# Windowed attention and a rational feed-forward layer: scores as 64x64 products, k and q turned on TensorE in the first steps, and a new order

## The chip, the cores and the metric

The kernel runs on one core of a Trainium2 chip. Time is device microseconds of one execution. A core has TensorE (PE: matrix products out of SBUF into PSUM; PEld is its weight load, which runs beside the products), VectorE (DVE), ScalarE (ACT), GpSimd (POOL) and the sync engine (SP). In this kernel POOL and SP mostly issue transfers: POOL's loads cast from f32 to bf16 on their way, SP issues transfers that transpose. TensorE's clock has two levels, 1.2 and 2.4 GHz; the profile shows the granted clock as a share of the higher one.

## The reference

```python
scores = (1 / sqrt(64)) * q @ k.T              # 4 batches, 8 heads, 768 tokens, 64 wide
keep = (key < 4) | ((0 <= query - key) & (query - key < 128))
a = softmax(where(keep, scores, -1e9))
x = (a @ v)                                    # put back to 3072 tokens x 512
h = x @ w_in                                   # 512 -> 2048
P = a0 + a1*h + a2*h*h + a3*h*h*h
Q = 1 + |b0|*|h| + |b1|*h*h
out = (P / (Q + 1e-6)) @ w_out                 # 2048 -> 512
```

Each query sees at most 128 keys behind it and the first 4 keys, the sink.

## The kernel before, in words

The 3072 tokens are worked in 12 steps of 256 tokens, three to a batch. A step `s` has an attention part and a feed-forward part; the two are apart by some steps, so that all engines have work.

**Attention.** k and q are held transposed, two heads (a pair, `i` = 0 to 3) on the 128 partitions. `scores(s, i)` makes, for each of the four blocks of 64 keys, one product with 192 queries behind it. The keys of the two heads stand block-diagonally in a 128x128 weight (`kT_fix`, half of it zeros), so that both heads come out of one product. For steps 0, 1, 2, 3, 6 and 9 (`PE_MASK`) a second product with the identity as weight adds the negative mask on two edges of 64 columns; in the other steps VectorE multiplies by a mask afterwards (`mask`). `exps` on ScalarE takes 768 columns per pair out of PSUM. There is one PSUM home for scores, `ps_scores` (step 0 borrows a second), so a group of scores waits for the exponentials of the group before. `sink_scores` makes the scores of the sink keys, `attend` the products with v (in 4 groups in step 0 and 3 groups later, called `G`), with a column of ones that gives the softmax sum; `normalize` (`norm`) divides on VectorE.

**How k, q and x are turned.** k and q of most steps are loaded by POOL (`load_k`, `load_q`) and transposed by SP transfers (`turn_k_tile`, `turn_q`). The transposed k lands in `kT_flat`, and VectorE copies it to the block-diagonal tile (`spread_k`, two instructions a step). In step 0 k and part of q are loaded as f32 by SP and ACT queues, cast, turned on TensorE and spread by VectorE and ScalarE; in step 1 k and q are turned on TensorE too. The normalized x is turned on TensorE in steps 0 and 1 (`turn_x`, `place_x`) and by SP transfers later (`turn_x_tile`). V stands in three tiles, one for each step of a batch, and POOL loads it with eight transfers a step.

**Feed-forward.** `project_in` (`gemm1`, four groups of 16 products of 256 columns a step), `copy_in` on ScalarE, and then the rational function on tiles of 4096 columns: `and`, `sqd`, `den`, `even`, `odd`, `odd_h`, `num`, `gate` on VectorE, `sqa`, `ln`, `exp` on ScalarE. Step 0 is worked in 2 parts, step 11 in 4. `project_out` (`gemm2`, four groups of 8 products of 512 columns), `copy_out`, `store`.

**Order.** Every piece of work has a number, and the list `ORDER` is the order in which the pieces are written into the program; each engine runs its pieces in that order. A negative number in the list is that many fillers (`spin`): products of the identity with itself into columns of `ps_scores` that nobody reads. There are 372 of them, 88 behind the first `gemm1` of step 2.

Of the kernel before, what the change touches and what calls it, by code (L numbers as in the profile page):

```python
# [72 lines left out]
def kernel(  # L73
# [13 lines left out]
    nc = tc.nc  # L87
# [20 lines left out]
    MW = NFFC * TS  # L108
    HW = MW // 2
    NQ0 = NTS + 1  # L110
    NS_PE = 2
    GRP = NPB // 2
    HG = H // 2
    CG = HG * D
# [139 lines left out]
    def load_v_sink():  # L254
        nc.scalar.dma_start(out=stage_s, in_=v[0, :, 0:NS, :])
# [791 lines left out]
```

## Time and profile before

| what | value |
|---|---|
| median of 3 runs | 271.79 us (270.04 to 273.13) |
| span of the profiled execution | 275.9 us |
| TensorE busy | 252.4 us (91%) |
| VectorE busy | 225.2 us (82%) |
| ScalarE busy | 221.2 us (80%) |
| GpSimd busy | 118.8 us (43%) |
| mean granted TensorE clock | 0.988 |

The profile shows one execution by its span from the first to the last instruction, and gives no other time for it. That span is 4.1 us longer than the median of the timed runs. Busy time of TensorE counts each product from its start to its modelled end, and neighbours overlap; how long a stream of products takes is read from the chain of waits, where a run of equal products stands with its length and count.

### The profile page before, as it was taken

Reading aid. Unit: us, or ns where it says so; the run is one execution under the profiler, and the core shown is the slowest. Engines: PE = TensorE matmul, PEld = TensorE weight load, DVE = VectorE, ACT = ScalarE, POOL = GpSimd, SP = SyncE. Lnnn points to the kernel's source line nnn. Section 1 sums busy time; section 2 is a strip of 40 time slices with the busy share of each in tenths; the row PEclk is TensorE's granted clock in tenths of the full one; section 3 lists DMA queues with packets and bytes.
Section 4 is the critical chain, followed back from the end, with each engine's and each line's share of the span. In section 5 each row is a group of like instructions: output and inputs, shape, how many; then the busy total and the mean of one; then the engine's idle time right before and its main releaser. Section 6 shows DMA issues by size and latency. Waiting matters only on the chain.

```text
span 275.9 us, 5692 instructions
## 1 busy us (share of the span) xinstructions
PE 252.4 (91%) x2344; PEld 192.4 (70%) x2344; DVE 225.2 (82%) x283; ACT 221.2 (80%) x201; POOL 118.8 (43%) x170
## 2 busy tenths in 40 slices
PE   2978898888599889999999999999999999999994
PEld 2968797777487587787776778777687776655551
DVE  3244318989917978999999999999999999999981
ACT  6084555898259669998989979999998999999870
POOL 8876677598069304083390990698000000000000
PEclk9997999999979999999999999999999999999999
DMA  6999999979999947599699999699901211211022
GB/s 140 192 162 185 117 112 129 137 85 162 118 79 90 124 74 53 130 105 180 80 74 154 124 110 203 45 139 156 122 4 39 77 57 21 76 76 40 26 88 77
DMA packets 113586, 28.72 MB, mean 104 GB/s; under 512 B 104344, under 2 KB 110488, under 8 KB 113560
## 3 DMA queue, kind: packets, MB, share of 16 engines
q0 software_dynamic: 75568, 13.00, 73.6%
q1 hardware_dynamic: 36464, 14.30, 28.8%
q10 hardware_dynamic: 1528, 1.06, 1.3%
q8 instruction: 18, 0.29, 0.5%
q14 instruction: 8, 0.07, 0.1%
HBM read 27.30 MB, written 6.29 MB: 122 GB/s over the span
## 4 chain that ended last, share of the span: by engine, by line
PE 51%; DVE 26%; ACT 12%; issue 6%; DMA 3%; POOL 1%; POOLq 0%
PE ps_out L664 19%; PE ps_h L596 16%; PE ps_s L432 5%; PE ps_o L524 4%; DMA xblk<-x_n 3%; DVE sq L634 3%; ACT lnq L640 3%; ACT e L480 3%; DVE kT L420 3%; DVE g L650 2%; PE ps_s L468 2%; DVE den L617 2%; DVE x_n L548 2%; ACT hb L603 2%; ACT den L645 2%
## 5 line engine op out<-in xcount | busy, mean ns | idle before, releaser
L596 PE MATMUL ps_h<-xblk,w_in_sb 128*128 128x256 bf16 x768 | 91.5, 276 | 2.6 <-DMA xblk<-x_n 2.5
L664 PE MATMUL ps_out<-w_out_sb,g 128*128 128x512 bf16 x368 | 86.3, 379 | 0.6 <-ACT o_t L673 0.3
L596 PEld LDWEIGHTS <-w_in_sb 128*128 128x128 bf16 x768 | 75.2, 99 | 13.5 <-issue 2.2
L238 POOL DMA_DIRECT2D v_bd<-in_v_dram x96 | 66.9, 723 | 37.1 <-PE ps_o L524 22.5
L664 PEld LDWEIGHTS <-g 128*128 128x128 bf16 x384 | 36.8, 98 | 37.2 <-issue 1.0
L603 ACT ACTIVATE hb<-ps_h 128x1024 bf16<-128x1024 f32 x48 | 48.9, 1033 | 12.9 <-PE ps_h L596 12.7
L480 ACT ACTIVATE e<-ps_s 128x768 bf16<-128x768 f32 x48 | 39.1, 816 | 11.9 <-PE ps_s L471 7.9
L640 ACT ACTIVATE lnq<-den,one_eps,qsc 128x4096 f32<-128x4096 bf16 (+2 forms) x16 | 47.2, 2956 | 0.0
L645 ACT ACTIVATE den<-lnq 128x4096 bf16<-128x4096 f32 (+2 forms) x16 | 44.1, 2771 | 0.0
L432 PE MATMUL ps_s<-ident 128*128 128x128 bf16 x372 | 28.1, 233 | 14.5 <-ACT e L480 9.3
L432 PEld LDWEIGHTS <-ident 128*128 128x128 bf16 x372 | 25.6, 106 | 16.7 <-issue 10.4
L230 POOL DMA_DIRECT2D k_bf<-in_k_dram x22 | 20.1, 916 | 35.5 <-DMA kT_flat<-k_bf 35.3
L524 PE MATMUL ps_o<-v_bd,e 128*128 128x130 bf16 x352 | 28.8, 220 | 1.2 <-DVE x_n L548 0.9
L650 DVE TENSOR_TENSOR g<-num,den 128x4096 bf16<-128x4096 bf16 (+2 forms) x16 | 28.0, 1752 | 1.6 <-ACT den L645 1.3
L468 PE MATMUL ps_s<-qT,kT 128*128 128x192 bf16 x192 | 28.1, 248 | 0.1
L621 DVE TENSOR_TENSOR den<-den,sq 128x4096 bf16<-128x4096 bf16 (+2 forms) x16 | 28.0, 1750 | 0.1
L634 DVE TENSOR_TENSOR sq<-sq,hb 128x4096 bf16<-128x4096 bf16 (+2 forms) x16 | 27.9, 1752 | 0.1
L637 DVE TENSOR_TENSOR num<-num,sq 128x4096 bf16<-128x4096 bf16 (+2 forms) x16 | 27.8, 1749 | 0.0
L524 PEld LDWEIGHTS <-e 128*128 128x128 bf16 x352 | 23.7, 97 | 5.2 <-DVE x_n L548 2.6
L610 ACT ACTIVATE sq<-hb 128x2048 bf16<-128x2048 bf16 (+1 forms) x15 | 25.4, 1695 | 0.1
L617 DVE TENSOR_SCALAR den<-hb 128x2048 uint32<-128x2048 uint32 (+2 forms) x16 | 15.9, 992 | 8.7 <-ACT hb L603 8.6
L222 POOL DMA_DIRECT2D q_bf<-in_q_dram x21 | 20.7, 996 | 0.4 <-DMA v_bd<-in_v_dram 0.4
(86 smaller groups left out, 252.4 us busy)
## 6 DMA issues: line engine op xcount, KB each, us to landing
out_dram<-o_t SPq DMA_DIRECT2D x22, 256.0 KB, 2.3
v_bd<-in_v_dram POOLq DMA_DIRECT2D x96, 32.0 KB, 4.6
k_bf<-in_k_dram POOLq DMA_DIRECT2D x22, 128.0 KB, 4.7
q_bf<-in_q_dram POOLq DMA_DIRECT2D x21, 128.0 KB, 5.2
w_in_sb<-in_moe_w_in_dram POOLq DMA_DIRECT2D x4, 512.0 KB, 7.8
w_out_sb<-in_moe_w_out_dram POOLq DMA_DIRECT2D x4, 512.0 KB, 8.1
stage_b<-in_q_dram ACTq DMA_DIRECT2D x2, 384.0 KB, 6.3
stage_a<-in_k_dram SPq DMA_DIRECT2D x2, 256.0 KB, 5.3
```

The costliest lines, as they stand in the source:

```text
L238: nc.gpsimd.dma_start(out=v_bd[s][e * 64:(e + 1) * 64, i, :, e, 0:D], in_=v[b, h, g * TS:(g + 1) * TS, :].rearrange("(j p) d -> p j d", p=64))
L432: nc.tensor.matmul(ps_scores[:, 0, 384:384 + P], lhsT=ident, rhs=ident, start=True, stop=True)
L468: nc.tensor.matmul(w_, lhsT=kT_fix[s % 2][:, i * NHF + n, :], rhs=qT_fix[b % 2][:, i, c:c + 192], start=True, stop=not on_pe)
L480: nc.scalar.activation(out=data.rearrange("p (a n) c -> p a n c", a=2), in_=ps[:, :, 0:384].rearrange("p a (n c) -> p a n c", n=2), func=A ...
L524: nc.tensor.matmul(ps_o[:, u, :], lhsT=l_, rhs=r_.rearrange("p e c -> p (e c)"), start=(m == 0), stop=(m == len(terms) - 1))
L596: nc.tensor.matmul(ps[:, n, :], lhsT=w_in_all[:, c, fc * P:(fc + 1) * P], rhs=xblk[m][:, c, :], start=(c == 0), stop=(c == NDMC - 1))
L603: nc.scalar.activation(out=hb[m][:, j * GW:(j + 1) * GW], in_=ps_h.pop((m, j)).rearrange("p n c -> p (n c)"), func=AF.Copy)
L634: nc.vector.tensor_tensor(out=sq[m][:, c], in0=sq[m][:, c], in1=hb[m][:, c], op=ALU.mult)
L640: nc.scalar.activation(out=lnq_fix[:, c], in_=den[m][:, c], func=AF.Ln, scale=qsc, bias=one_eps)
L645: nc.scalar.activation(out=den[m][:, c], in_=lnq_fix[:, c], func=AF.Exp, scale=-1.0)
L650: nc.vector.tensor_tensor(out=g_of[m][:, c], in0=num[m][:, c], in1=den[m][:, c], op=ALU.mult)
L664: nc.tensor.matmul(ps_out[m, tt], lhsT=g_of[m][:, co:co + P], rhs=w_out_all[:, fc, :], start=(fc == 0), stop=(fc == NFFC - 1))
```

## The change

- **Scores.** A group of scores, `scores(s, k)`, now covers two pairs and half of the keys: four blocks of 64 keys for four heads on 2 x 2 quarters of the array. Each head has its own 64x64 weight and product of 192 columns, so 8 products a group instead of 4, and in the steps with masks on TensorE 8 mask products with a 64x64 part of the identity instead of 4. Function `side` says on which half of the PSUM partitions a head comes out. The sink's scores are made by four weights of 32 columns that come out on four strips of partitions. Weights, rows and columns of v change to match.
- **No spreading.** `kT_fix` has three tiles that hold k as it comes out of the transposition; SP's transfers write it directly. `spread_k`, `spread_k0`, and the clearing of the block-diagonal tiles are gone.
- **k and q of steps 0 to 2** are turned on TensorE (`KQ_PE = 3`), out of loads that give each partition two or three tokens that follow each other (`load_kc`, `load_qc`); q of step 0 comes by POOL and no longer by ACT's queue with a cast. `place_kc` and `place_qc` put the tokens in order.
- **x of steps 0 to 3** is turned on TensorE (`X_PE = 4`), placed by VectorE or ScalarE as the table `ENGINE` says, in the PSUM bank of the table `BANK`.
- **V** has one tile for the whole batch; the second and third step of a batch are loaded by one set of eight transfers, which waits until the step before both has been attended.
- Step 0 of the feed-forward part is worked in 4 parts (`PARTS0`).
- **Order and fillers.** `ORDER` is new throughout, and has 4 fillers in one place, which use a tile of ones. On TensorE it begins: q of step 0 in two groups, 4 fillers, k of step 0 in two groups, q of step 1, `scores(0, 0)`, k of step 1, then the other scores of step 0 and `attend` of step 0, with k of step 2 and the four groups of scores of step 1 between them; the first `gemm1` of step 0 stands behind `scores(1, 0)`. The first `gemm1` of step 2 stands behind two groups of scores of step 3, the other two and the first `gemm2` group of step 0 behind it (before, all four and that group stood ahead of it). On VectorE `placed_x(2, 0)` stands behind most of step 0's rational function. On POOL q of step 0 is the second piece and q of step 1 the sixth; `load_v` of steps 4 and 5 begins with three transfers that stand ahead of the loads of q and k of step 4.

```diff
-    NS_PE = 2
+    KQ_PE = 3
+    X_PE = 4
+    PARTS0 = 4
...
+    ENGINE = {('cast_k0', 1): 'ACT',
...
+               ('placed_x', 0, 0): 'DVE',
+               ('placed_x', 1, 0): 'DVE',
+               ('placed_x', 2, 0): 'DVE',
+               ('placed_x', 2, 1): 'DVE',
+               ('placed_x', 3, 1): 'DVE'}
...
+    BANK = {('turn_k0', 0): 'ps_o',
...
+             ('turn_x', 2, 0): 'ps_m',
+             ('turn_x', 3, 0): 'ps_h',
+             ('turn_x', 3, 1): 'ps_m'}
...
+    v_all = const_pool.tile([P, GPB * NHF * VW], BF16, name="v_bd")
...
-    kT_fix = [const_pool.tile([P, NPB * NHF, P], BF16, name=f"kT_{n}") for n in range(2)]
-    KW = P + 2 * NS
-    k_sink = [const_pool.tile([P, NPB * KW], BF16, name=f"k_sink_{n}") for n in range(2)]
+    kT_fix = [const_pool.tile([P, NPB, TS], BF16, name=f"kT_{n}") for n in range(3)]
+    SR = P // NPB
...
+    def side(e, i):
+        lo = 64 * ((e + i) % 2)
+        return slice(lo, lo + 64)
...
+    def load_kc(s):
+        b, g = divmod(s, GPB)
+        k_raw[s] = a_kv.tile([P, H, NTS, D], BF16, tag="k_raw", name="k_raw")
+        nc.gpsimd.dma_start(
+            out=k_raw[s].rearrange("p h t d -> p h (t d)"),
+            in_=k[b, :, g * TS:(g + 1) * TS, :].rearrange("h (p t) d -> p h (t d)", t=NTS))
+
+    def load_qc(s):
+        n0, nt = q_tiles(s)
+        b, T = divmod(n0, S // P)
+        q_raw[s] = a_kv.tile([P, H, 3, D], BF16, tag="q_raw", name="q_raw")[:, :, 0:nt, :]
+        nc.gpsimd.dma_start(
+            out=q_raw[s],
+            in_=q[b, :, T * P:(T + nt) * P, :].rearrange("h (p t) d -> p h t d", t=nt))
...
-    def load_v(s, h):
+    def load_v(s, h, steps):
         b, g = divmod(s, GPB)
-        v_bd[s] = v_fix[s % 3]
         i, e = divmod(h, 2)
         nc.gpsimd.dma_start(
-            out=v_bd[s][e * 64:(e + 1) * 64, i, :, e, 0:D],
-            in_=v[b, h, g * TS:(g + 1) * TS, :].rearrange("(j p) d -> p j d", p=64))
+            out=v_half[side(e, i), g * NHF:(g + steps) * NHF, i, e, 0:D],
+            in_=v[b, h, g * TS:(g + steps) * TS, :].rearrange("(j p) d -> p j d", p=64))
...
+    def turned(bank, pairs, nt, raw):
+        ps = full_bank(bank).bitcast(BF16)[:, 0:len(pairs) * nt * P]
+        ps = ps.rearrange("p (i t c) -> p i t c", i=len(pairs), t=nt)
+        for il, i in enumerate(pairs):
+            for t in range(nt):
+                for rows, t_ in raw(i, t):
+                    nc.tensor.transpose(ps[rows, il, t, :], t_, ident)
+        return ps.rearrange("p i t c -> p i c t")
+
+    def of_head(t_):
+        return lambda i, t: [(slice(e * 64, (e + 1) * 64), t_[:, 2 * i + e, t, :])
+                             for e in range(2)]
...
+    def copy(eng, dst, src):
+        if eng == "ACT":
             nc.scalar.activation(out=dst, in_=src, func=AF.Copy)
         else:
             nc.vector.tensor_copy(out=dst, in_=src)
...
+    def place_kc(s, grp, eng):
+        pairs = pairs_of(grp)
+        copy(eng, kT_fix[s % 3][:, pairs[0]:pairs[-1] + 1, :].rearrange(
+            "p i (c t) -> p i c t", t=NTS), kT_flat.pop((s, grp)))
...
     def turn_k_tile(s, t):
-        if s not in kT_flat:
-            kT_flat[s] = a_kv.tile([P, NPB, TS], BF16, tag="kT_flat", name="kT_flat", bufs=3)
-        nc.sync.dma_start_transpose(out=kT_flat[s][:, :, t * P:(t + 1) * P], in_=k_bf[s][:, t, :])
-
-    def spread_k(s):
-        src = kT_flat.pop(s)
-        for e in range(2):
-            lo, hi = e * 64, (e + 1) * 64
-            nc.vector.tensor_copy(out=kT_fix[s % 2][lo:hi, :, lo:hi],
-                                  in_=src[lo:hi].rearrange("p i (j c) -> p (i j) c", c=64))
-        if s % GPB == 0:
-            copy_k_sink(s // GPB)
-
-
+        nc.sync.dma_start_transpose(out=kT_fix[s % 3][:, :, t * P:(t + 1) * P],
+                                    in_=k_bf[s][:, t, :])
...
-            nc.tensor.matmul(ps_scores[:, 0, 384:384 + P], lhsT=ident, rhs=ident, start=True,
+            nc.tensor.matmul(ps_scores[:, 0, 384:384 + P], lhsT=warm, rhs=warm, start=True,
                              stop=True)
...
-            nc.tensor.matmul(ps[:, c0:TS], lhsT=k_sink[b % 2][:, i * P:(i + 1) * P],
+            rows = slice(i * SR, (i + 1) * SR)
+            nc.tensor.matmul(ps[rows, c0:TS], lhsT=k_sink[b % 2][:, rows],
                              rhs=qT_fix[b % 2][:, i, g * TS + c0:(g + 1) * TS],
-                             start=(i == 0), stop=(i == NPB - 1))
+                             start=True, stop=True)
...
-    def spare_psum(s, i):
-        return s == 0 and i % 2 == 1
-
-    def scores(s, i):
+    def spare_psum(s, k):
+        return s == 0 and k % 2 == 1
+
+    def scores(s, k):
         b, g = divmod(s, GPB)
+        grp, half = divmod(k, 2)
         ps = ps_scores
-        if spare_psum(s, i):
+        if spare_psum(s, k):
             ps = ps_hp.tile([P, 2, 512], FP32, tag="ps_h", name="ps_s0")
-        for n in range(NHF):
-            c = g * TS + 64 * n
-            w_ = ps[:, n // 2, (n % 2) * 192:(n % 2) * 192 + 192]
-            on_pe = s in PE_MASK
-            nc.tensor.matmul(w_, lhsT=kT_fix[s % 2][:, i * NHF + n, :],
-                             rhs=qT_fix[b % 2][:, i, c:c + 192], start=True, stop=not on_pe)
-            if on_pe:
-                nc.tensor.matmul(w_.rearrange("p (m c) -> p m c", c=64)[:, 0:3:2, :], lhsT=ident,
-                                 rhs=nege0 if g == 0 and n == 0 else nege, start=False, stop=True)
-        ps_e[s, i] = ps
-
-    def exps(s, i):
-        grp, il = divmod(i, 2)
-        e_t = e_fix[grp, s % 2]
-        ps = ps_e.pop((s, i))
-        data = e_t[:, 64:].rearrange("p (j c) -> p j c", c=EW)[:, il * NHF:(il + 1) * NHF, 0:192]
-        nc.scalar.activation(out=data.rearrange("p (a n) c -> p a n c", a=2),
+        on_pe = s in PE_MASK
+        for n in range(2):
+            for il in range(2):
+                i, j = 2 * grp + il, 2 * half + n
+                c = g * TS + 64 * j
+                for e in range(2):
+                    rows = slice(e * 64, (e + 1) * 64)
+                    nc.tensor.matmul(ps[side(e, i), il, n * 192:(n + 1) * 192],
+                                     lhsT=kT_fix[s % 3][rows, i, j * 64:(j + 1) * 64],
+                                     rhs=qT_fix[b % 2][rows, i, c:c + 192],
+                                     start=True, stop=not on_pe)
+            for il in range(2) if on_pe else ():
+                blocks = ps[:, il, n * 192:(n + 1) * 192].rearrange("p (m c) -> p m c", c=64)
+                neg = nege0 if g == 0 and half == n == 0 else nege
+                for e in range(2):
+                    rows = slice(e * 64, (e + 1) * 64)
+                    nc.tensor.matmul(blocks[side(e, il), 0:3:2, :], lhsT=ident[rows, rows],
+                                     rhs=neg[rows], start=False, stop=True)
+        ps_e[s, k] = ps
...
+        if s % GPB < 2:
+            n = 1 + s % GPB
+            old = [("ones", m_) for m_ in range(s, s + n)] if s < 3 else (
+                [("attended", s - 3)] + [("attend", s - 2, G) for G in groups(s - 2)][:-1]
+                if n == 1 else [("attended", s - 3), ("attended", s - 2)])
+            for h in range(H):
+                piece(("load_v", s, h), "POOL", 0.65 if n == 1 else 0.75, r_ + 1.0,
+                      lambda s=s, h=h, n=n: load_v(s, h, n), old, kind="sw", load=0.3 * n)
...
-            if s < NS_PE:
-                piece(("turn_x", s, part), "PE", 0.4, r_, lambda s=s, part=part: turn_x(s, part),
-                      norms, takes="ps_h")
-                piece(("placed_x", s, part), "ACT", 0.57, r_, lambda s=s, part=part: place_x(s, part),
-                      [("turn_x", s, part)] + free, frees="ps_h")
+            if s < X_PE:
+                nm = ("turn_x", s, part)
+                bank = bank_of(nm, "ps_h" if s == 0 else "ps_o")
+                piece(nm, "PE", 0.4, r_, lambda s=s, part=part, bank=bank: turn_x(s, part, bank),
+                      norms, takes=bank)
+                np_ = ("placed_x", s, part)
+                eng = eng_of(np_, "ACT")
+                piece(np_, eng, 0.57, r_, lambda s=s, part=part, eng=eng: place_x(s, part, eng),
+                      [nm] + free, frees=bank)
...
-        return 4 if m == LAST else 2 if m == 0 else 1
+        return 4 if m == LAST else PARTS0 if m == 0 else 1
```

## Rows read from the trace of the kernel before

**Rows 1.** Busy time by stage: PE, PEld, DVE, ACT, POOL, granted clock, DMA, GB/s
```profile
33.10:65.85 32.75, 28.94 (x357) 26.46 (x356) 22.41 (x34) 24.27 (x25) 25.16 (x36) 1.00 1.61 119
65.85:75.38 9.53, 5.61 (x67) 4.44 (x67) 9.35 (x8) 4.77 (x6) 2.48 (x3) 1.00 1.77 133
75.38:120.00 44.62, 42.36 (x381) 32.52 (x381) 33.75 (x37) 36.18 (x29) 18.51 (x25) 0.96 0.98 93
120.00:190.00 70.00, 69.90 (x635) 52.88 (x634) 69.19 (x71) 65.28 (x55) 44.79 (x58) 1.00 1.28 125
190.00:255.00 65.00, 64.61 (x510) 44.89 (x508) 63.62 (x59) 62.36 (x49) 2.86 (x5) 1.00 0.43 61
255.00:276.00 21.00, 16.67 (x98) 8.21 (x96) 14.04 (x26) 11.72 (x14) 0.00 (x0) 1.00 0.16 63
```

**Rows 2.** TensorE's groups of instructions from 120 to 190 us
```profile
L596 PE MATMUL ps_h<-xblk,w_in_sb 128*128 128x256 bf16 x256 | 30.2, 273 | 0.0
L664 PE MATMUL ps_out<-w_out_sb,g 128*128 128x512 bf16 x114 | 27.0, 379 | 0.0
L524 PE MATMUL ps_o<-v_bd,e 128*128 128x130 bf16 x122 | 10.0, 219 | 0.1
L468 PE MATMUL ps_s<-qT,kT 128*128 128x192 bf16 x64 | 9.2, 246 | 0.0
L524 PE MATMUL ps_o<-v_sink,e_sink 128*128 128x130 bf16 x28 | 6.1, 219 | 0.0
L471 PE MATMUL ps_s<-nege,ident 128*128 128x128 bf16 x32 | 5.1, 219 | 0.0
L440 PE MATMUL ps_sink<-qT,k_sink 128*128 128x128 bf16 (+1 forms) x16 | 2.0, 246 | 0.0
```

**Rows 3.** Chain of waits, 195 to 245 us: start, length, what
```profile
197.76 0.33 PE ps_s L468 x4
198.09 0.44 PE ps_sink L440 x4
198.53 1.73 PE ps_out L664 x8
...
204.05 0.85 PE ps_o L524 x15
...
216.76 3.49 PE ps_h L596 x32
```

**Rows 4.** Chain of waits, the front up to 76 us
```profile
2.01 0.41 POOL q_bf L222
...
5.16 9.08 PE ps_s L432 x113
...
21.82 0.85 PE ps_t L408 x8
...
24.77 0.82 ACT e L480
...
25.63 0.24 PE ps_s L468
...
40.42 0.83 DVE den L617
...
65.85 9.48 DMA xblk<-x_n
```

**Rows 5.** Granted clock (share behind POOL) and engines, two single microseconds
```profile
20.00:21.00 1.00, 0.00 (x0) 0.00 (x0) 0.00 (x0) 0.98 (x2) 1.00 (x3) 0.94 1.09 181
21.00:22.00 1.00, 0.88 (x9) 0.87 (x9) 0.49 (x2) 0.45 (x2) 1.00 (x3) 0.50 1.26 201
```

**Rows 6.** VectorE's groups from 120 to 190 us, spreading of k and reciprocal
```profile
L420 DVE COPY kT<-kT_flat 64x1024 bf16<-64x1024 bf16 x10 | 6.1, 609 | 0.1
...
L536 DVE RECIPROCAL rec<-ps_o 128x6 f32<-128x6 f32 (+1 forms) x11 | 2.4, 214 | 0.2 <-PE ps_o L524 0.2
```

**Rows 7.** DMA issues of the first 20 us: KB each, median us to landing
```profile
q_bf<-in_q_dram POOLq DMA_DIRECT2D x3, 128.0 KB, 6.8
```

More of the change, by code (lines that the diff above doesn't have):

```diff
@@ L702, in on_act, with eng_of, bank_of, halves @@
         return fixed + cols / 1200.0
-    def if_step(s, *name):
-        return name + (s,) if 0 <= s < NSTEP else None
+    def eng_of(name, default="DVE"):
+        return ENGINE.get(name, default)
+    def bank_of(name, default):
+        return BANK.get(name, default)
+    def halves(s, what):
+        return (0, 1) if s == 0 or what == "q" and q_tiles(s)[1] == 3 else (None,)
+    def k_free(s):
+        return [("scores", s - 3, i) for i in range(NPB)] + (
+            [("k_sink", (s - 3) // GPB)] if (s - 3) % GPB == 0 else []) if s >= 3 else []
@@ L707, with q_free @@
+    def q_free(s):
+        b = s // GPB
+        return [w_ for s_ in range(GPB * (b - 2), GPB * (b - 1))
+                for w_ in [("sink_scores", s_)] + [("scores", s_, i) for i in range(NPB)]
+                ] if b >= 2 else []
     for grp in range(GRP):
-        piece(("load_k0", grp), "SP", 0.5, -40 + grp, lambda grp=grp: load_k0(grp), kind="hw",
-              load=1.0)
-        piece(("load_q0", grp), "ACT", 0.5, -40 + grp, lambda grp=grp: load_q0(grp), kind="hw",
-              load=1.0)
+        piece(("load_k0", grp), "ACT" if grp else "SP", 0.5, -40 + grp,
+              lambda grp=grp: load_k0(grp), kind="hw", load=1.0)
@@ L807 @@
-    for n in range(2 * NS_PE + 1, NQT):
-        s = (n - 1) // NTS
-        b, T = divmod(n, S // P)
-        last = [w_ for s_ in range(GPB * (b - 2), GPB * (b - 1))
-                for w_ in [("sink_scores", s_)] + [("scores", s_, i) for i in range(NPB)]
-                ] if b >= 2 else []
-        piece(("turn_q", n), "SP", 1.25, 4 * s - 14, lambda n=n: turn_q(n), [("load_q", n)] + last,
-              kind="hw", load=0.4, lat=0.8)
+        bank = bank_of(("turn_k0", grp), "ps_o" if grp else "ps_m")
@@ L816, in q_ready @@
+    for s in range(KQ_PE, NSTEP):
+        n0, nt = q_tiles(s)
+        for n in range(n0, n0 + nt):
+            piece(("turn_q", n), "SP", 1.25, 4 * s - 14, lambda n=n: turn_q(n),
+                  [("load_q", n)] + q_free(s), kind="hw", load=0.4, lat=0.8)
+    q_home = {}
+    for s_ in range(NSTEP):
+        n0_, nt_ = q_tiles(s_)
+        for n_ in range(n0_, n0_ + nt_):
+            q_home[n_] = s_
     def q_ready(n, i):
-        if n < NQ0:
-            return ("place_q0", i)
-        return ("place_q" if n < 2 * NS_PE + 1 else "turn_q", n)
+        s = q_home[n]
+        if s >= KQ_PE:
+            return ("turn_q", n)
+        return ("place_qc", s, None if len(halves(s, "q")) == 1 else i // 2)
@@ L821, in v_loads @@
     def v_loads(s):
-        return [("load_v", s, h) for h in range(H)]
+        return [("load_v", s - (s % GPB == 2), h) for h in range(H)]
     for s in range(NSTEP):
         b, g = divmod(s, GPB)
-        if s == 0:
-            pass
-        elif s < NS_PE:
-            piece(("turned_k", s), "PE", 0.6, 4 * s - 18, lambda s=s: turn_k2(s),
-                  [("load_k", s, t) for t in range(NTS)] + [("ident",)], takes="ps_m")
-        else:
+        if s >= KQ_PE:
             for t in range(NTS):
@@ new lines, in k_ready @@
+        def k_ready(s, grp):
+            if s == 0:
+                return [("place_k0", grp)]
+            if s < KQ_PE:
+                return [("place_kc", s, None)]
+            return [("turn_k", s, t) for t in range(NTS)]
+        if g == 0:
+            piece(("k_sink", b), "DVE", 0.2, 4 * s - 10 if b else -20, lambda b=b: copy_k_sink(b),
+                  k_ready(s, 0) + k_ready(s, 1) + [("clear_ks", b % 2)]
+                  + ([("sink_scores", GPB * (b - 2) + g_) for g_ in range(GPB)] if b >= 2 else []))
@@ L871, with e_ready @@
             both = [("exps", s, 2 * grp), ("exps", s, 2 * grp + 1)]
-            if s in PE_MASK:
-                piece(("mask", s, grp), "NONE", 0.0, 0, None, both)
-            else:
+            if s not in PE_MASK:
                 piece(("mask", s, grp), "DVE", 0.68, NPB * s + 2 * grp + 1 - 7 - 0.05,
                       lambda s=s, grp=grp: mask(s, grp), both + [("edges",)])
+        def e_ready(s, n, i):
+            grp = i // 2
+            if s not in PE_MASK:
+                return [("mask", s, grp)]
+            return [("exps", s, 2 * grp + h) for h in range(n + 1)]
         gs = list(groups(s))
```

317 lines of the change are left out of this document (150 added, 167 removed), and 94 rows, old and new, of the table ORDER.

## The prediction

> **What bounds the kernel now.** I read the busy time by stage first. The bounds of the stages are the first `gemm1` (33.1 us), the last `norm` of step 2 (65.85), the first `gemm1` of step 2 (75.38), and round times after it [rows 1]. From 120 to 190 us TensorE shows 69.90 of 70.00 us busy and VectorE 69.19, ScalarE 65.28 [rows 1]. Since busy time of TensorE overlaps, I check it against the rate at which it streams, read off the chain of waits: 32 `gemm1` products in 3.49 us (109 ns each), 8 of `gemm2` in 1.73 (216), 15 of `attend` in 0.85 (57), 4 score products in 0.33 (82), 4 sink products in 0.44 (110) [rows 3]. A mask product has 128 columns, and `attend`'s 130, so 57 ns as well. With the counts of that stage: 256 x 0.109 + 114 x 0.216 + 150 x 0.057 + 64 x 0.082 + 32 x 0.057 + 16 x 0.110 = 27.9 + 24.6 + 8.6 + 5.2 + 1.8 + 1.8 = 69.9 us [rows 2, 3]. So TensorE has no gap there: it is the bound, VectorE is 1% behind it, ScalarE 7%. From 75.38 us on there are 640 `gemm1`, 376 `gemm2`, 324 `attend`, 128 score, 32 mask and 32 sink products left; that is 185 us by the same rates (the sinks at their full width), of the 200.5 us to the end of the span.
>
> Ahead of 75.38 us it is different. In the first 33.1 us TensorE has some 8 us of real work (28 `attend`, 24 score and 24 mask products, 44 turned blocks at about 57 ns); 9.08 us are one row of 113 fillers [rows 4]. From 33.1 to 75.38 us it has 128 x 0.109 + 8 x 0.216 + 80 x 0.057 + 40 x (0.082 + 0.057) + sinks and turned blocks = 27.5 us of 42.3. The largest single loss is the transfer that turns x of step 2: 9.48 us from the last `norm` to the first `gemm1` [rows 4]. So the change can win at the front, and from 75 us on only by what it takes off TensorE.
>
> **The front, up to the first gemm1 (now 33.1 us).** q of step 0 is POOL's second piece; the first load left at 2.01 us before, and q loads of the first 20 us took 6.8 us to land [rows 4, 7], so it is there at about 9. At the lower clock a turned block took 0.85 / 8 = 0.106 us [rows 4]. 24 blocks of q, 8 of k and 16 of q of step 1 stand ahead of the first scores: 5.1 us, to 14; a placement in between brings it to about 15. Then ScalarE sets the pace: each group of exponentials takes 0.82 us [rows 4], seven of them, a placement of k, one of x and a sink's stand ahead of the last group of scores, 5.7 + about 2, so the first `gemm1` comes near 24. Without fillers the clock will often be at its lower level: between 20 and 21 us TensorE ran nothing, and in the next microsecond the clock was at 0.50, the lower level, fillers or not [rows 5]. Eight masked score groups at half rate are 8 x 0.56 = 4.5 us longer. I take 28, that is **5.1 us earlier**; the ends are 24 and 34.
>
> **From there to the first gemm1 of step 2 (now 42.3 us).** x of step 2 is now turned by 8 blocks on TensorE and two copies on VectorE, whose nearest row is the spread at 0.61 us [rows 6]. The 9.48 us are gone; next late is VectorE's queue, since `placed_x(2, 0)` stands behind step 0's rational function. VectorE was busy 22.41 us up to 65.85 [rows 1]. Off it go four spreads (4 x 0.61 = 2.4) and half a `num` (0.6); onto it three copies of x (1.8), a placement of q (0.6), a quarter of the squares (0.6), and 14 more instructions by the division into four parts. A reciprocal of 6 columns takes 0.214 us in all [rows 6]; that and 0 bound the start of one, I take 0.1: 1.4 us. Sum 23.8 us. Before, VectorE began at 40.42 [rows 4] and was busy 22.41 of 25.4 us; at that share 23.8 become 27.0. It begins one `gemm1` group (1.75) and one copy later than the first `gemm1`, about 3 us, not 7.3. With the last copy that is 30.6 us, **11.7 less**. TensorE's 27.5 us fit in barely; ends 28 and 38.
>
> **From there to the end (now 200.5 us).** Moved behind the mark: one `gemm2` group (1.7), two masked score groups (2 x 0.56 = 1.1), 8 turned blocks of x (0.5). Taken off: 88 fillers, 88 x 0.057 = 5.0 us, of which I count half, as some stood in waits. The granted clock of 0.96 from 75 to 120 us [rows 1] followed on the wait for x, and is worth 0.04 x 44.6 = 1.8 us; gone with it.
> The price of **64x64 products** no row shows, as all products of before are 128x128. A step has twice as many of the same columns. Four at a time they cost half of now, one at a time double. From the mark on, that is 12.3 us now (128 x 0.082 + 32 x 0.057): -6.2 or +12.3. I take two at a time, no change: the products of now come every 57 ns at best, weight load included [rows 3], and doubling their number speaks against the half. Going from one shape of product to another and back, ten times a step, can cost from 0 to 0.16 us each time: a first product on an idle array took 0.24 us instead of 0.082 [rows 3, 4]. I take 0.04, since the change finds the queue filled: 80 x 0.04 = 3.2, end 12.8.
> The Trainium skill speaks against even that: TensorEngine Tiling (Array Packing), "Key Properties", says that changing the tiling mode drains TensorE, and "Restrictions and Gotchas" that different row tiles cannot use one PSUM bank at the same time. Here the two heads of a pair write to one bank from different halves of the rows. No run here shows either; by both, the sum would be that of the slower rival.
> VectorE loses its spreads, 6.1 of 70 us [rows 6]; with TensorE as the bound that is slack and no gain. The direct transposition into `kT_fix` is the same transfer as before: nothing. POOL issues 32 fewer loads of v; it was busy 43% and waits for nobody who counts: nothing, as long as the order of its loads holds (below).
> Sum: 200.5 + 1.7 + 1.1 + 0.5 - 2.5 - 1.8 + 3.2 = 202.7, **2.2 more**.
>
> **Sum.** -5.1 - 11.7 + 2.2 = -14.6 us of the span of 275.9. The span stands 4.1 us above the median of the timed runs, and I take the difference over: 271.8 - 14.6 = **257 us**.
>
> **The rivals.**
> *Four at a time.* The small products overlap fully and the change of shape is free: -6.2 - 3.2, and the sinks' four strips run together, about -1: 247 us. ScalarE has 36.2 + 65.3 + 62.4 + 11.7 = 175.6 us from 75 us on [rows 1], below TensorE's 180 or so, so it wouldn't stop this. For it: the four quarters share no row and column pair. Against: the weight loads double. The Trainium skill, TensorE: Matmul & The Clock Gate, "Part 3", reports such overlap (3.07 times with four row tiles); it would give this rival's time. Chance 0.18.
> *The clock at the front.* Without the fillers TensorE is at half clock until the feed-forward part fills it. The front's real work of 8 us and more turned blocks then takes 8 us longer and is the path: 265 us. For it [rows 5]; against, ScalarE paces that stretch. Chance 0.15.
> *One at a time, with a drain.* The other sign: each 64x64 product runs alone, and the array empties at each change of shape. From the mark on +12.3 and 80 x 0.12 = 9.6; in the masked steps 0 to 3 16 groups x 0.56 = 9 and 40 x 0.12 = 4.8, of which half on the path, 7. Together 286 us, slower by 5%. It decides from 14.6 us on, which is the doubled price and 0.03 us more a change of shape. For it: TensorE has no gap from 120 us on, so all of it shows. Chance 0.13.
> *Late loads of step 4.* `load_v` of step 4 now waits for all of `attend` of step 2, and the loads of q and k of step 4 queue behind it on POOL, then SP's transpositions behind those. A load lands in some 7 us and a transposition took up to 9.48 [rows 4, 7]; the two `gemm` parts between (7 + 6.9 us) just cover that. If not, some 13 us are given back at the start of the full stage and nothing is won: 270 us. Chance 0.10.
>
> **How the numbers follow.** The forecast has 0.44, with 250 to 263 as its own range. A difference of 1% (2.7 us) is about what a measurement can tell here. Faster by over 1%: 0.44 + 0.18 + 0.15 = 0.77; within 1%: 0.10; slower: 0.13. The range leaves out the slower rival and little else; it goes from 244 (the fast rival with a front of 24 us) to 274.
>
> **What would show it.** The first `gemm1` near 28 us, the first one of step 2 near 59, no transfer of x ahead of it. From there TensorE without gaps, and a group of unmasked scores at 0.33 us in the chain of waits; 0.17 or 0.66 decide for the rivals. VectorE some 9% below TensorE. I am wrong if the score groups take over 0.6 us, if ScalarE rather than TensorE fills the middle, or if the clock stays below 1.00 past 40 us.

## The result and the profile after

The changed kernel took **259.3 us** (median of 4 runs, 257.2 to 260.4) beside 272.5 us for the kernel before in the same session (270.0 to 275.3): ratio 0.955, 95% interval 0.946 to 0.964. 257 was forecast. The profiled execution took 260.1 us, its span is 258.0.

The transfer of x that stood ahead of step 2 [rows 4] is gone, and the sum of the three stretches came out at -17.9 us of span, where -14.6 was forecast:

| from - to | before | forecast | after |
|---|---|---|---|
| start - first `gemm1` | 33.1 | 28 | 26.1 |
| first `gemm1` - first `gemm1` of step 2 | 42.3 | 30.6 | 32.3 |
| from there to the end of the span | 200.5 | 202.7 | 199.6 |

Executions over 1.5% above a kernel's fastest count as slow and stay out of the ratios, and the profiled one of the kernel before was such a one. Time and span of this kernel differ by 1.7 us (272.29 beside 270.6 in one execution), so a span of 275.9 means some 277.6 us, an estimate, 5 us above the median. This is why the spans differ by 17.9 us and the medians by 13.2 only, and the column "before" holds some 5 us too much. Two runs that share its instructions tell where they can lie. Experiment 1 has the same order up to the first `gemm1` and reached it at 30.9 us, not 33.1. Experiment 4 has the same order from there on and took 38.9 us to the first `gemm1` of step 2 and 198.9 to the end, not 42.3 and 200.5. So up to 2, 3 and 2 us of the three numbers belong to that one execution, and the gains read from the table are upper bounds.

The first `gemm1` of step 2 is found by counting: a step has four groups of 16 products, so it is the ninth group. The `gemm1` rows of TensorE's timeline of the changed kernel, other rows left out, with the wait ahead in brackets:

```profile
26.09 1.92 PE L625 MATMUL ps_h<-xblk,w_in_sb 128*128 128x256 bf16 x16
30.41 3.16 PE L625 MATMUL ps_h<-xblk,w_in_sb 128*128 128x256 bf16 x16 [2.40 <-DMA w_in_sb<-in_moe_w_in_dram]
34.39 1.91 PE L625 MATMUL ps_h<-xblk,w_in_sb 128*128 128x256 bf16 x16
36.65 1.92 PE L625 MATMUL ps_h<-xblk,w_in_sb 128*128 128x256 bf16 x16 [0.35 <-DMA w_in_sb<-in_moe_w_in_dram]
45.32 3.20 PE L625 MATMUL ps_h<-xblk,w_in_sb 128*128 128x256 bf16 x16
49.42 1.91 PE L625 MATMUL ps_h<-xblk,w_in_sb 128*128 128x256 bf16 x16
52.02 1.91 PE L625 MATMUL ps_h<-xblk,w_in_sb 128*128 128x256 bf16 x16
55.96 1.91 PE L625 MATMUL ps_h<-xblk,w_in_sb 128*128 128x256 bf16 x16
58.37 1.92 PE L625 MATMUL ps_h<-xblk,w_in_sb 128*128 128x256 bf16 x16
```

Two things stand here that the forecast had not put in this stretch: the second group waits for `w_in`, and two groups run 1.25 us longer than their neighbours, at the lower clock: it was 0.50 from 32 to 34 us and 0.51 from 46 to 48. The busy time by stage says the same, and shows where the machine is not full (PE, PEld, DVE, ACT, POOL, granted clock, DMA share, GB/s), as in [rows 1]:

```profile
26.09:58.37 32.28, 27.19 (x344) 21.77 (x337) 21.87 (x49) 22.43 (x27) 22.66 (x32) 0.89 1.93 132
70.00:84.00 14.00, 10.75 (x90) 6.91 (x88) 11.24 (x9) 9.62 (x9) 5.05 (x8) 0.88 2.20 116
84.00:130.00 46.00, 45.63 (x492) 31.23 (x491) 42.35 (x46) 43.03 (x38) 22.39 (x27) 1.00 1.46 120
130.00:200.00 70.00, 69.99 (x712) 47.08 (x710) 68.43 (x65) 67.64 (x59) 20.94 (x25) 1.00 0.99 108
```

From 70 to 84 us TensorE has only 10.75 of 14 us and its clock is at 0.88; from 130 to 200 all three compute engines are within 4% of full. TensorE's groups of that stretch answer to [rows 2]:

```profile
L625 PE MATMUL ps_h<-xblk,w_in_sb 128*128 128x256 bf16 x261 | 31.0, 273 | 0.0
L492 PE MATMUL ps_s<-qT,kT 64*64 64x192 bf16 x136 | 6.3, 255 | 0.0
L501 PE MATMUL ps_s<-nege,ident 64*64 64x128 bf16 x32 | 1.5, 216 | 0.0
```

261 `gemm1` products in 70 us; before it was 256 [rows 2]. So the steady pace is at most 2% higher. The chain of waits, start, length and what (the lines that answer to [rows 3] and [rows 4]):

```profile
26.20 10.39 DMA w_in_sb<-in_moe_w_in_dram
...
69.93 9.30 DMA kT<-k_bf
79.28 0.54 PE ps_s L492 x8
79.81 2.99 PE ps_h L625 x16
...
98.32 2.29 DVE den L650
100.61 2.20 DVE num L666
...
104.02 2.20 DVE g L679
...
130.49 0.29 PE ps_s L492 x8
130.78 0.22 PE ps_sink L460 x4
131.00 1.83 PE ps_out L693 x8
132.84 0.85 PE ps_o L553 x15
133.69 1.75 PE ps_h L625 x16
...
145.23 1.85 PE ps_h L625 x16
...
158.44 0.21 PE ps_s L492 x4
158.65 0.06 PE ps_s L501 x4
158.70 0.08 PE ps_s L492 x4
158.78 0.06 PE ps_s L501 x4
158.84 1.83 PE ps_out L693 x8
```

**What a 64x64 group costs.** A group without masks stands with 0.29 us, but the `gemm` group right behind it is always 0.10 longer (1.85 for 1.75, 1.83 for 1.73): 0.39 in all, before 0.33 [rows 3]. With masks it is 0.21 + 0.06 + 0.08 + 0.06 = 0.40 (the rounded rows give 0.41; the starts, 158.44 and 158.84, give 0.40) and again 0.10 behind it: 0.50, before 0.33 + 4 x 0.057 = 0.56. These two groups separate the price of the products from that of the change of shape. One at a time, 8 score products are 8 x 0.082 = 0.66 us and 8 masks 8 x 0.057 = 0.46. With p the share of that price which is paid, taken to be the same for both kinds, and c a change there and back: 0.66p + c = 0.39 and 1.12p + c = 0.50. So p = 0.24 and c = 0.23: **four at a time, and about 0.11 us for each change of shape.** The rows show it directly: the second four score products of a masked group pass in 0.08 us, the price of one.

**VectorE on the chain.** From 96 to 126 us nearly every row of the chain is VectorE's; three of them are shown. There it is the bound, not TensorE.

### The profile page after: what moved, and what is told of

It is laid out like the page before. It is cut to its first block, busy times and chain, and to the rows that moved or that the text cites. A ratio compares the mean times of both kernels' runs of the same rounds, so it can differ in the third digit from the quotient of the medians.

```text
span 258.0 us, 5619 instructions
## 1 busy us (share of the span) xinstructions
PE 229.9 (89%) x2332; PEld 155.1 (60%) x2332; DVE 219.3 (85%) x294; ACT 216.9 (84%) x196; POOL 98.9 (38%) x136
## 4 chain that ended last, share of the span: by engine, by line
PE 56%; DVE 17%; DMA 10%; ACT 8%; issue 5%; ACTq 2%; POOL 0%; DVEq 0%
PE ps_h L625 23%; PE ps_out L693 21%; PE ps_o L553 8%; DMA w_in_sb<-in_moe_w_in_dram 7%; DMA kT<-k_bf 4%; PE ps_s L492 3%; DVE den L650 3%; ACT den L674 3%; DVE num L666 2%; DVE g L679 2%; DVE x_n L577 2%; DVE den L646 2%; ACT lnq L669 1%; ACTq L294 1%; DVE sq L663 1%
## 5 line engine op out<-in xcount | busy, mean ns | idle before, releaser
L276 POOL DMA_DIRECT2D v_bd<-in_v_dram x64 | 47.0, 751 | 46.8 <-PE ps_o L553 36.9
L669 ACT ACTIVATE lnq<-den,one_eps,qsc 128x4096 f32<-128x4096 bf16 (+1 forms) x18 | 47.9, 2667 | 1.3 <-DVE den L650 1.3
L674 ACT ACTIVATE den<-lnq 128x4096 bf16<-128x4096 f32 (+1 forms) x18 | 44.8, 2492 | 0.1
L679 DVE TENSOR_TENSOR g<-num,den 128x4096 bf16<-128x4096 bf16 (+1 forms) x18 | 28.3, 1571 | 0.7 <-ACT o_t L702 0.5
L650 DVE TENSOR_TENSOR den<-den,sq 128x4096 bf16<-128x4096 bf16 (+1 forms) x18 | 28.3, 1574 | 0.5
L663 DVE TENSOR_TENSOR sq<-sq,hb 128x4096 bf16<-128x4096 bf16 (+1 forms) x18 | 28.4, 1576 | 0.3
L666 DVE TENSOR_TENSOR num<-num,sq 128x4096 bf16<-128x4096 bf16 (+1 forms) x18 | 28.3, 1573 | 0.1
L492 PE MATMUL ps_s<-qT,kT 64*64 64x192 bf16 x384 | 19.1, 261 | 4.7 <-DMA kT<-k_bf 3.2
L577 DVE SCALAR_TENSOR_TENSOR x_n<-ps_o,ratio,rec 128x384 bf16<-128x384 f32 (+1 forms) x33 | 18.9, 573 | 1.2
L655 DVE TENSOR_SCALAR num<-sq,acoef 128x4096 bf16<-128x4096 bf16 (+1 forms) x18 | 18.1, 1017 | 0.8 <-ACT sq L639 0.7
```

Source lines behind the costliest of these rows:

```text
L276: nc.gpsimd.dma_start(out=v_half[side(e, i), g * NHF:(g + steps) * NHF, i, e, 0:D], in_=v[b, h, g * TS:(g + steps) * TS, :].rearrange("(j ...
L650: nc.vector.tensor_tensor(out=den[m][:, c], in0=den[m][:, c], in1=sq[m][:, c], op=ALU.add)
L663: nc.vector.tensor_tensor(out=sq[m][:, c], in0=sq[m][:, c], in1=hb[m][:, c], op=ALU.mult)
L666: nc.vector.tensor_tensor(out=num[m][:, c], in0=num[m][:, c], in1=sq[m][:, c], op=ALU.add)
L669: nc.scalar.activation(out=lnq_fix[:, c], in_=den[m][:, c], func=AF.Ln, scale=qsc, bias=one_eps)
L674: nc.scalar.activation(out=den[m][:, c], in_=lnq_fix[:, c], func=AF.Exp, scale=-1.0)
```

## The experiments

**Theories.** Theory A, at first: the gain is the wait for x that was taken away (with the fillers a small part), VectorE's dropped spreads give nothing, the late loads of step 4 give some of it back. Rivals: the fillers were a cost of their own; VectorE sets the pace with TensorE. Ratios are to the kernel before in the same session. Differences from the changed kernel are those of medians out of different sessions; by the ratios the 7.7 us of experiment 2 are 6.1, the 9.0 of experiment 6 are 8.1, and the 3.1 of experiment 9 are 4.6.

**1. The kernel before with x of steps 2 and 3 turned on TensorE** (`b_x4`), and the placements and first `gemm1` of step 2 moved behind it:

```diff
-            if s < NS_PE:
+            if s < 4:
                 piece(("turn_x", ...
 ORDER
+turn_x(2, 0), placed_x(2, 1), placed_x(2, 0), gemm1(2, 0)      (15 fillers out)
```

> The kernel before, with x of steps 2 and 3 turned on TensorE and placed by ScalarE, the first gemm1 group of step 2 moved right behind that, and 15 fillers between them left out. Theory (the gain is made ahead of the first gemm1 of step 2, mostly by the missing transfer of x): that gemm1 starts some 8 us earlier, near 67 us, the granted clock stays at 1.00 there, and the run is 6 to 9 us faster than before, near 264. Rival (the gain is that of the 64x64 products and the missing spreads, in the full stage): what is gained at the front is waited out later, less than 2 us faster.

Measured: 277.9 us (276.5 to 279.5), ratio 1.018 (1.010 to 1.027). The first `gemm1` of step 2 came at 66.3 us, 9 us earlier, of which 2.2 stand already at the first `gemm1`. But in the rows of TensorE and then of ScalarE

```profile
30.90 1.91 PE L595 MATMUL ps_h<-xblk,w_in_sb 128*128 128x256 bf16 x16
...
66.26 3.44 PE L595 MATMUL ps_h<-xblk,w_in_sb 128*128 128x256 bf16 x16 [2.88 <-ACT xblk L579]
...
76.08 1.02 ACT L602 ACTIVATE hb<-ps_h 128x1024 bf16<-128x1024 f32 x1
```

the group takes 3.44 us, and its output is copied only 10 us after its start, as ScalarE's order was left as it was. The 9 us were given back. In this arrangement taking the transfer away gains nothing; that doesn't price it.

**2. The changed kernel with x of steps 2 and 3 by transfers** (`a_x2`):

```diff
-    X_PE = 4
+    X_PE = 2
```

> The changed kernel with x of steps 2 and 3 turned by SP's transfers again, as before. Theory: the first gemm1 of step 2 waits for the transfer and starts 6 to 10 us later, and the run is 5 to 9 us slower than the changed kernel, near 266. Rival (fillers and products carry the gain): within 2 us of the changed kernel, near 260.

Measured: 267.0 us (266.2 to 272.1), ratio 0.977 (0.970 to 0.985): 7.7 us slower than the changed kernel. The first `gemm1` of step 2 came 5.1 us later, less than the 6 to 10 expected, and with step 3's there are two waits in TensorE's timeline, each with a group at nearly double length behind it:

```profile
63.43 3.56 PE L624 MATMUL ps_h<-xblk,w_in_sb 128*128 128x256 bf16 x16 [6.88 <-DMA xblk<-x_n]
...
87.08 3.42 PE L624 MATMUL ps_h<-xblk,w_in_sb 128*128 128x256 bf16 x16 [4.83 <-DMA xblk<-x_n]
```

In the new order this part is worth 7.7 us; the two groups alone are 3.1 us longer than at 1.92 each.

**3. The kernel before without any of its 372 fillers** (`b_nospin`):

```diff
 ORDER
-    ... -113, ... -14, ... -15, ... (all 27 negative entries)
```

> The kernel before with all 372 fillers left out. Theory: the fillers mostly stand in waits; within 3 us of before, 269 to 275, with a lower clock at the front and the first scores a little earlier. Rival (leaving out the fillers is the gain): 8 us or more faster, under 264.

Measured: 264.6 us (264.1 to 265.2), ratio 0.969 (0.963 to 0.976), granted clock 1.00 in the profiled execution and 0.979 to 1.00 in all four. The theory that the fillers are worth 3 us at most fell: taking them out gives 8 to 9 us, two thirds of the whole gain. The busy time by stage, cut at the first `gemm1` and the first of step 2:

```profile
0.00:27.41 27.41, 13.49 (x128) 11.80 (x129) 13.54 (x53) 16.62 (x27) 20.55 (x40) 1.00 1.34 164
27.41:62.98 35.57, 28.69 (x314) 24.61 (x312) 25.63 (x37) 28.23 (x29) 26.38 (x36) 1.00 1.59 123
```

33.1 became 27.4, and 42.3 became 35.6 (beside the 30.9 and 38.9 of experiments 1 and 4 the two differences are 3.5 and 3.3 us). The transfer of x was still there, with the same work ahead of it, but it was quicker. DMA issues, here from 54 to 64 us and in experiment 4 from 58 to 70:

```profile
xblk<-x_n SPq DMA_TRANSPOSE x2, 3.7
...
xblk<-x_n SPq DMA_TRANSPOSE x2, 6.5
```

Where the kernel before shows 9.48 us [rows 4], x of step 2 landed here at 60.6 us, before TensorE was through the scores that stand ahead of its `gemm1`. So 9.48 us was no fixed price.

**4. The kernel before without its first 113 fillers only** (`b_nofirst`):

```diff
 ORDER
-    ... -113, ...
```

> The kernel before without its first 113 fillers, the other 259 left in. If the fillers cost by holding up the first turned blocks (first block at 14 us, the q load there by some 10): 4 to 5 us faster than before, near 268, and the rest of the 9 us is in the later fillers. If the clock that they keep up is worth what they cost: within 1 us of before. If the later fillers cost it all: within 1 us as well, with the first gemm1 earlier and the first gemm1 of step 2 where it was.

Measured: 268.3 us (267.8 to 268.7), ratio 0.984 (0.978 to 0.990). The first `gemm1` comes at 29.2 us, 3.9 earlier than in the profile of before and 1.7 earlier than in experiment 1. The stretch behind it, whose order is that of before:

```profile
29.19:68.10 38.91, 34.09 (x422) 30.79 (x421) 27.47 (x38) 28.21 (x29) 30.38 (x42) 1.00 1.61 132
```

By the times, the first row of fillers costs some 4 us and the other 259 another 4.

**5. Without fillers, and with x of steps 2 and 3 on TensorE** (`b_nospin_x4`), now with `copy_in` and `gemm1` of step 2 put between the score groups on both engines:

```diff
-            if s < NS_PE:
+            if s < 4:
 ORDER (without fillers)
+turn_x(2, 0), placed_x(2, 1), placed_x(2, 0), sqa(1, 0), scores(3, 2), gemm1(2, 0), exps(3, 2),
+copy_in(2, 0), sink_scores(3), scores(3, 1), gemm1(2, 3), exps(3, 1), copy_in(2, 3), ...
```

> The kernel before without fillers, with x of steps 2 and 3 turned on TensorE, placed ahead of the squares of step 1, and the first two gemm1 groups of step 2 with their copies put between the scores of step 3, as in the new order. Theory now (fillers that hold TensorE up, some 9 us, and the transfer of x, some 5, make the gain between them): 258 to 261, like the changed kernel. Rival (the new order, the small products or the loads of step 0 to 2 are needed as well): 263 to 266, like the kernel before without fillers.

Measured: 266.9 us (265.4 to 268.2), ratio 0.979 (0.971 to 0.986); the theory that fillers and transfer make the whole gain fell. The first `gemm1` of step 2 came 3.0 us earlier than in experiment 3, at 60.0, and the rest took 4.9 longer; from 60 to 120 us TensorE waits 2.1 us for ScalarE's placement of x and 1.4 for a `norm`. So what is worth 7.7 us in the new order gained nothing in this arrangement of the old one, where ScalarE places x of step 2 and not VectorE. That no arrangement of the old order would keep the 3.0 us isn't shown.

**6. VectorE's work put back** (`a_spread`): in steps 3 to 11 of the changed kernel four copies more a step.

```diff
     def normalize(s, G):
+        if s >= 3 and G == 0:
+            for e in range(4):
+                rows = slice(e % 2 * 64, e % 2 * 64 + 64)
+                nc.vector.tensor_copy(out=spare[rows], in_=w_in_all[rows, e, 0:512])
```

> The changed kernel with VectorE given the work of the dropped spreads again: four copies of 64x512 from a weight tile to a spare one in each of steps 3 to 11, some 1.3 us a step, 12 in all. If TensorE alone is the bound (the prediction): under 3 us slower than the changed kernel. Rival (VectorE is a bound beside it, so the dropped spreads are what pays for the change of shape): 7 to 11 us slower, near 268.

Measured: 268.3 us (267.9 to 269.2), ratio 0.984 (0.977 to 0.992): 9.0 us slower than the changed kernel. The stretch from 130 to 200 us, and the copies as a group of VectorE:

```profile
130.00:200.00 70.00, 65.71 (x654) 44.51 (x661) 68.44 (x78) 62.92 (x54) 21.05 (x25) 1.00 1.03 105
```

```profile
L561 DVE COPY spare<-w_in_sb 64x512 bf16<-64x512 bf16 x32 | 10.3, 322 | 0.8
```

VectorE has the same 68.4 us, and TensorE falls from 69.99 to 65.71 (32 of the 36 copies are in the window of the row, 84 us to the end; `spare` is a new tile). TensorE's longest wait from 84 to 200 us is for VectorE, and none is for a load of GpSimd's:

```profile
PE ps_o L553 <- DVE x_n L581: 4.8, 4, 1.4
```

36 copies of 0.32 us are 11.6 us, and 9.0 of them come out at the end: in the new order VectorE is a bound.

**7. The spreads taken off VectorE in the old order** (`b_nospin_tiny`):

```diff
+            w = 64 if s < 3 else 2
-            nc.vector.tensor_copy(out=kT_fix[s % 2][lo:hi, :, lo:hi],
-                                  in_=src[lo:hi].rearrange("p i (j c) -> p (i j) c", c=64))
+            nc.vector.tensor_copy(out=kT_fix[s % 2][lo:hi, :, lo:lo + w],
+                                  in_=src[lo:hi].rearrange(...)[:, :, 0:w])
```

> The kernel before without its 372 fillers, whose spreads of k for steps 3 to 11 copy only 2 of each 64 columns (the scores of those steps are then taken with keys of earlier steps; everything else runs). Without the edit it took 264.6 us, and its 16 spreads after 75 us are 8.1 us of VectorE at 506 ns. Theory (VectorE shares the bound with TensorE in the old order too, so the spreads that the change drops are part of its gain): 257 to 260 us. Rival (in the old order TensorE alone sets the pace, and the dropped spreads give something only with the new order): 263.5 to 265.5 us.

Measured: 262.7 us (260.2 to 263.4), ratio 0.964 (0.955 to 0.974), beside 0.969 in experiment 3. It lies between the two expectations: 1.9 us by the medians, 1.3 by the ratios, and the intervals overlap, so that neither nothing nor some more is excluded. The rows of experiment 3 and then of this one:

```profile
62.98:120.00 57.02, 50.19 (x447) 37.48 (x445) 50.15 (x54) 49.00 (x39) 35.23 (x42) 1.00 1.64 131
120.00:190.00 70.00, 69.99 (x623) 53.08 (x622) 69.23 (x73) 65.28 (x58) 40.97 (x53) 1.00 1.18 119
...
64.80:120.00 55.20, 52.10 (x470) 39.95 (x468) 48.99 (x54) 49.59 (x40) 33.13 (x40) 1.00 1.49 135
120.00:190.00 70.00, 70.00 (x625) 52.52 (x623) 67.22 (x74) 66.56 (x57) 40.71 (x53) 1.00 1.18 115
```

From 120 us on VectorE falls from 69.23 to 67.22, and TensorE is full in both, with 128x128 scores as before: there the relief gives nothing. Ahead of 120 us TensorE had gaps, 6.8 us in experiment 3 and 3.1 here. In all, this execution took 195.7 us from the first `gemm1` of step 2 to the end, 4.5 less than experiment 3, and lost 2.4 of them ahead of it, where its granted clock was 0.91. So by this one execution the old order does gain where TensorE isn't full.

**8. q and k of step 4 loaded ahead of everything that stands before them on GpSimd** (`a_loads4`):

```diff
 ORDER, GpSimd's pieces
+load_q(9), load_q(10), load_k(4, 1), load_k(4, 0)
 load_v(4, 3), load_w_out(3), load_v(4, 1), load_vss(6), load_w_out(2), load_v(4, 2)
-load_q(9), load_q(10), load_k(4, 1), load_k(4, 0)
```

> The changed kernel with the four loads of q and k of step 4 moved ahead of the first loads of v of step 4 on POOL, so that they no longer queue behind the wait for attend of step 2. Theory (the rival of the prediction about late loads holds in part): the wait of TensorE of 3.25 us for the turned k of step 4 and the half clock behind it go; 3 to 5 us faster than the changed kernel, near 255. Rival (VectorE sets the pace there and the wait is hidden): within 1 us of the changed kernel.

Measured: 260.1 us (258.7 to 261.1), ratio 0.952 (0.945 to 0.959): no change. The wait for k went, and another came in its place, since `load_vss` now stands behind (TensorE's timeline):

```profile
68.30 0.27 PE L552 MATMUL ps_o<-v_sink,e_sink 128*128 128x130 bf16 x1 [4.99 <-DMA v_sink<-in_v_dram]
```

**9. Only the three loads of v moved** (`a_v4late`):

```diff
 ORDER, GpSimd's pieces
-load_v(4, 3), load_v(4, 1), load_v(4, 2)      (each among the loads of w_out and v_sink)
 load_w_out(3), load_vss(6), load_w_out(2), load_q(9), load_q(10), load_k(4, 1), load_k(4, 0)
+load_v(4, 3), load_v(4, 1), load_v(4, 2)
```

> The changed kernel with only the first three loads of v of step 4 moved behind the loads of q and k of step 4, so that weights and sinks are not pushed back as they were when the q and k loads were moved ahead. Theory (the late k of step 4 costs): 2 to 4 us faster than the changed kernel, near 256. Rival (VectorE's queue is next late there): within 1 us.

Measured: **256.2 us** (254.8 to 258.6), ratio 0.938 (0.930 to 0.946), 3.1 us below the changed kernel and the lowest median of all that were run; the intervals of the two ratios touch at 0.946. GpSimd's timeline of the changed kernel shows what held it:

```profile
54.74 0.69 POOL L276 DMA_DIRECT2D v_bd<-in_v_dram  x1 [4.33 <-PE ps_o L553]
...
58.96 2.42 POOL L239 DMA_DIRECT2D q_bf<-in_q_dram  x2
61.37 1.79 POOL L269 DMA_DIRECT2D k_bf<-in_k_dram  x2
```

and that of this one what came of it:

```profile
55.00 0.89 POOL L268 DMA_DIRECT2D k_bf<-in_k_dram  x1
```

k leaves 6.4 us earlier, and TensorE's wait of 3.2 us ahead of step 4's scores is gone, with the lower clock behind it (0.88 from 70 to 84 us, now 1.00; from 56 to 70 it is now 0.89, where it was 1.00).

**10. That, and the fourth V tile cleared earlier** (`a_clearv4`), `clear_v0(3)` moved to right behind `clear_v0(1)` on VectorE:

```diff
 ORDER, VectorE's pieces
+clear_v0(1), clear_v0(3)
```

> The changed kernel with the three V loads of step 4 behind its k load on GpSimd (alone: 256.2 us), and with the clearing of the fourth V tile moved forward on VectorE to right behind that of the second, so that GpSimd doesn't stand 4.6 us at 9.5 us with loads behind it. Theory (the stall delays what the front needs): first gemm1 1 to 4 us earlier than 26.1 us, and 252 to 255 us. Rival (the front waits for w_in, whose loads come no sooner when the transfers of V begin earlier and share the DMA engines with it): first gemm1 within 0.5 us or later, and 255.5 to 257.5 us.

Measured: 258.1 us (254.3 to 260.3), ratio 0.939 (0.928 to 0.949), by the ratio the same as experiment 9; the first `gemm1` at 25.9 us. The edit did not take the wait away (GpSimd's waits up to 40 us):

```profile
POOL v_bd L275 <- DVE v_bd L204: 4.8, 1, 4.8
```

so what that stall costs stays open.

**11. Neighbouring products in different PSUM banks** (`a_bank`):

```diff
-            for il in range(2):
-                for e in range(2):
+            for il, e in ((0, 0), (1, 1), (0, 1), (1, 0)):
```

> The changed kernel with the products of a score group in another order: neighbours write different PSUM banks, where in the changed kernel the two heads of a pair write the same bank one after the other; the two heads' row halves now come as 0, 1, 1, 0 in place of 0, 1, 0, 1. Theory (a shared bank doesn't hold two products apart here; a group of eight takes 0.29 us because the eight run two at a time): group unchanged at 0.29 us or, as every second neighbour is now of the same row half, up to 0.45 us, and the time 258 to 262 us. Rival, the rule of the Trainium skill, TensorEngine Tiling (Array Packing), Restrictions and Gotchas, that products of different row tiles can't write one PSUM bank at the same time: the group falls below 0.25 us and the time by 1.5 to 4 us, to 255 to 258 us.

Measured: 259.5 us (258.3 to 259.6), ratio 0.953 (0.947 to 0.959). Its chain of waits has the same group:

```profile
128.76 0.29 PE ps_s L490 x8
```

Neither order nor bank matters, as the theory's number had it; but its reason, two at a time, fell with the masked groups above: all four quarters already run together, with both heads of a pair writing one bank.

## Why the prediction was right, and where its steps were not

**The front** (-5.1 forecast, -7.0 measured). The first `gemm1` came at 26.1 us, between the 24 of ScalarE's pace and the 28 that I took. But the step gave the gain to a new way of bringing in k and q, and never asked what the fillers cost there. Without fillers the old front alone ends at 27.4 us (experiment 3). Of the 7.0 us 5.7 are to be had without the new loads; beside the 30.9 us of experiment 1 it is 3.5 of 4.8.

**The stage up to step 2** (-11.7 forecast, -10.0 measured, and -6.6 beside the 38.9 us of experiment 4). The step counted on all of the 9.48 us of the transfer; the same transfer took 6.5 us in experiment 4 and 3.7 in experiment 3, so that -11.7 came close to the table by the luck of one execution. VectorE was not next late all through: 21.87 of 32.28 us busy, against the 23.8 of 27.0 worked out. Two waits for `w_in` (2.4 and 0.35 us) and two groups at half clock (2 x 1.25 us) are what stands in its place, 5.3 us in all. Here too the fillers hid in the sum: they make 6.7 of the 10.0 us in the old order, or 3.3 of the 6.6. Turning x on TensorE is worth 7.7 us in the new order (experiment 2) and gained nothing in the arrangement of experiment 5: it is no term that can be added by itself.

**The rest** (+2.2 forecast, -0.9 measured, and +0.7 beside the 198.9 us of experiment 4). "Two at a time, no change" and "0.04 us a change of shape" were both wrong, in opposite directions. From the mark on 128 x 0.082 + 32 x 0.057 = 12.3 us became half; a change there and back costs 0.23 us for each of 32 groups, 7.4; and the sinks fell from 0.44 to 0.22 us, 8 times. -6.2 + 7.4 - 1.8 = -0.6 us, where +3.2 was forecast. That is 3.8 us less than the forecast, but the late loads of step 4, which it put at nothing, took 3.1 back (experiment 9). The two make -0.7 us; the stretch came out 3.1 below its forecast, or 1.5 beside experiment 4, and the remainder has no price. No run has the changed kernel with 128x128 scores, so the -0.6 is worked out from rows and not tested. The Trainium skill, TensorEngine Tiling (Array Packing), "Key Properties", has the array drain when the tiling mode changes: these runs agree in that each change costs about 0.11 us. The same page of the Trainium skill, "Restrictions and Gotchas", bars different row tiles from one PSUM bank at the same time; here two heads on different row halves write one bank, and four products pass in 0.08 us, the time of one. TensorE: Matmul & The Clock Gate, "Part 3", of the Trainium skill, is nearer to that with its overlap of packed products: the overlap is there, but not the 247 us of that rival, since the change of shape takes it back.

**"With TensorE as the bound that is slack and no gain"**: this step failed. VectorE was 1% behind TensorE, I had written so myself, and it needs no more than that for both to count. The sign that it would end some 9% below TensorE didn't come: it was at 68.43 of 70 us beside 69.99, 2% below. In the new order, 11.6 us of work put back on it cost 9.0 (experiment 6). In the old order taking work off it gives about 2 us (experiment 7), as TensorE fills the stage from 120 us on with or without that. That the smaller products and the lighter VectorE need each other fits this, but is argued and not shown.

**The rivals.** *Late loads of step 4* did not take all of the gain, as its 270 us had it, but it came: 3.1 us (experiment 9). *The clock at the front* came too, but behind the first `gemm1`: two groups at half clock (3.16 and 3.20 us for 1.92) in the second stretch, and one (2.99 for 1.75) behind the late k, some 3.8 us in place of the 8. With it came a sign that I had named for being wrong, a clock below 1.00 past 40 us: it was 0.51 from 46 to 48 us and 0.88 from 70 to 84. *One at a time* was refuted by the first score group. *Four at a time* holds for the products and fails as a forecast.

So the total was right with partly wrong reasons and some luck: costs that the sum had left out stood against gains that it had left out. Without fillers the old order has 264.6 us; the rest, 5.3 us by the medians and 4.0 by the two ratios, is what x on TensorE, less VectorE work, the products, the new loads and the new order give together, less what the loads of `w_in` and of step 4 take back. How these few us divide among the parts can't be said: x on TensorE and VectorE's work are each worth much in the new order and little in the old, and the others were not tried apart.

## What to carry to other kernels

A filler stands in the queue ahead of real work; take all of them out once and time it, before any of them is called free. When two engines are within a few per cent of full, a relief of one alone shows little (here 2 us of 8.1) and work put on it shows for the most part (9.0 of 11.6): cost both sides, and test a part by taking it out of the new kernel as well as by putting it into the old one. When a load waits for a buffer, look at what is queued behind it on the same issuing engine, and move the load, not its followers. Compare the stretches of two profiles only after checking each span against the median of the timed runs: here one profile was 5 us above it, and two runs with the same instructions showed where that can lie.

## What the runs showed that I had not expected

- The kernel before ran faster without its fillers, and its granted clock hardly fell: 0.979 to 1.00 in four executions without the 372 (experiment 3), 0.985 to 1.00 in seven with them in the same session.
- Four 64x64 products of 192 columns on the four quarters of the array took 0.08 us, as long as one 128x128 product; each change between that shape and the full one took about 0.11 us. For groups of 8 that makes 0.39 us for 0.33; with 8 masks more, 0.50 for 0.56: a 64x64 score product saves 0.082 / 4 = 0.02 us, so by this estimate the change of shape pays from some 11 products a group on.
- Four sink products of 256 columns on strips of 32 columns took 0.22 us, entry included, before 0.44.
- The same transposing transfer of x took 9.4 us in one run and 3.7 in another (medians of two, before and experiment 3), with nothing changed but the fillers.
